# One weight tile of a decode kernel, loaded in 16 pieces of 1 to 15 and 8 partitions

## The chip, the cores and the metric

The kernel runs on one core of one Trainium2 chip. The metric is the device time of one execution in microseconds (us). Three runs of the kernel before gave 1349.16, 1345.97 and 1348.38 us; their median is 1348.38 us. In the text PE is TensorE, PEld its weight load, DVE VectorE, ACT ScalarE, POOL GpSimd and SP SyncE, whose queue issues nearly all DMAs of this kernel. A DMA is carried out by the core's 16 DMA engines.

## The reference

One decode step of a transformer block for two sequences: attention against a cache of 8192 positions, then a bilinear feed-forward block. All tensors are float32. Cut to what matters:

```python
# B, D, H, Sk, Dh, F = 2, 448, 16, 8192, 256, 1792
q = (layernorm(x) @ wq).reshape(B, 1, H, Dh).transpose(0, 2, 1, 3)
p = softmax(einsum("bhqd,bhkd->bhqk", q, k_cache) * Dh ** -0.5)
o = einsum("bhqk,bhkd->bhqd", p, v_cache)
h = x + o.transpose(0, 2, 1, 3).reshape(B, 1, H * Dh) @ wo
out = h + ((layernorm(h) @ w_gate) * (layernorm(h) @ w_up)) @ w_down
```

The two caches hold 2 x 16 x 8192 x 256 numbers each, 537 MB together. They are read once.

## The kernel before, in words

The loop over `i` takes the 32 pairs of a head `h` and a sequence `b` one after the other (`h, b = divmod(i, 2)`). Each step reads two tiles of K (`k_h_b_0`, `k_h_b_1`) and two of V (`v_h_b_0`, `v_h_b_1`). Such a tile has 128 partitions with 32 KB each, 4 MB in all. The four tiles of a step live in four buffers (`ring`), so a tile of step `i` takes the buffer of the same tile of step `i - 1`: a K tile can be issued when DVE has scanned the K tile before it, a V tile when PE has multiplied with the V tile before it.

DVE scans each K tile with 32 multiply-and-sum instructions (L203) against the query, which stands broadcast on all partitions. The softmax of the 8192 scores goes over PE, DVE and ACT in small instructions (L212 to L227: `m`, `mT`, `nm`, `nb_ps`, `p`, `l_ps`, `rl`). PE then multiplies the 64 columns of `p` with the two V tiles (L234, `o_ps`; 16 products of two columns for each tile), and projects the head's result into `acc_ps` (L252).

The weights come by head pairs: `w_hp` holds, for two heads, the rows of `wq` and `wo`, as 128 partitions with 3584 numbers (14,336 bytes) each, 1.8 MB in all. `load_w` (L138) fetches one; there are two buffers for it. `w_0` is loaded first of all, and `w_{hp+1}` is issued in the step in which `hh == 1 and b == 0`, between that step's K loads and its V loads (L195). The last one, `w_7`, belongs to step 26 (`h` = 13, `b` = 0). The queries of the next head pair are computed from it in the same step by 10 matmuls, which the trace shows as 20 (L173 and L178, `queries`), and are first needed in step 28.

All loads of K, V and weights go through SP's one queue in program order. SP issues a load and goes on; where a load has to wait (for its buffer, or for a counter), SP waits, and everything behind it in the program waits too. The scheduler gives each load one of eight completion counters (`DMAHW0` to `DMAHW7`), in turn, and a load is not issued until the load that had the same counter before it, eight loads earlier, has landed. The order of PE's, DVE's and ACT's instructions is set by the scheduler from the program. After the loop, `wg_t`, `wu_t` and `wd_t` (the feed-forward weights, 6.9 MB, in the freed buffers) are loaded, and a tail of PE, DVE and ACT work of some 10 us follows the landing of `wu_t`.

Of the kernel before, what the change touches and what calls it, by code (L numbers as in the profile page):

```python
# [13 lines left out]
B, D, H, SK, DH, F = 2, 448, 16, 8192, 256, 1792  # L14
EPS = 1e-5
P = 128
# [9 lines left out]
FG = (512, 512, 384, 384)  # L26
FO = (0, 512, 1024, 1408)
NF = F // P

LAYOUT = (  # L30
    (slice(0, P), slice(0, DC - 1), slice(0, DC - 1)),
# [6 lines left out]
def tile_decode_block(  # L38
# [18 lines left out]
    nc = tc.nc  # L57
# [79 lines left out]

    def load_w(hp):  # L138
        t = wpool.tile([P, WQ + WO], F32, tag="w", name=f"w_{hp}")
        nc.sync.dma_start(t, wqo[hp])  # L140
        return t

    def load_cache(src, b, h, c, name):
# [3 lines left out]
        return t  # L147

    w_now = load_w(0)

    xT = transposed(x_sb, "x")
# [39 lines left out]
    for i in range(H * B):  # L191
        h, b = divmod(i, B)
        hp, hh = divmod(h, 2)
        kt = [load_cache(k_cache, b, h, c, "k") for c in range(NCH)]
        if hh == 1 and b == 0 and hp + 1 < H // 2:  # L195
            w_next = load_w(hp + 1)
# [63 lines left out]
    def load_ff(w, name):  # L260
        t = ring.tile([P, NF * D], F32, tag="ring", name=name)
        nc.sync.dma_start(t, w)
        return t
# [3 lines left out]

    wd_t = ring.tile([P, NF, D], F32, tag="ring", name="wd_t")
    at = 0
# [60 lines left out]
    for g in range(4):  # L330
        for n in range(FG[g] // P):
            for q in range(DC):
                nc.tensor.matmul(  # L333
                    y_ps[32 * q : 32 * q + B, : DW[q]], hmT[:, n, g, :],
                    wd_t[:, k, q * P : q * P + DW[q]],
                    start=False, stop=(k == NF - 1),
                )
# [14 lines left out]
def pack(np, inputs):  # L352
# [20 lines left out]
    a = np.asarray(inputs["B_w_down"])  # L373
    got["wd"] = a.reshape(NF, P, D).transpose(1, 0, 2).reshape(P, NF * D)
    return {k: np.ascontiguousarray(v) for k, v in got.items()}
# [25 lines left out]
```

## Time and profile before

| | us |
|---|---|
| runs: lowest, median, highest | 1345.97, 1348.38, 1349.16 |
| the profiled execution: its span, first to last instruction | 1345.7 |
| PE busy | 496.5 |
| DVE busy | 741.2 |
| ACT busy | 60.6 |
| moved from memory | 561.2 MB, a mean of 418 GB/s |

The profiled execution has a span of 1345.7 us; no other time of it is given, and its span lies 2.7 us under the median of the runs. The profile page shows the busy time of each engine, the span in 40 slices, the DMA queues, the chain of work that ended last, and the costliest groups of instructions. Apart from the page, the trace answers questions: the chain in order of time, the instructions of one engine in a stretch of time, and, for given stretches, each engine's busy time with the mean busy share of the 16 DMA engines and the rate that they reached in GB/s. One DMA engine of 16 is a share of 0.0625.

### The profile page before, as it was taken

How to read it: one execution, taken by the hardware profiler on the slowest of the kernel's cores; microseconds unless marked ns; L12 is line 12 of the kernel's file. 1: busy time of each engine (PE TensorE's matmuls, PEld its weight loads, DVE VectorE, ACT ScalarE, POOL GpSimd, SP SyncE). 2: the span in 40 equal slices, each digit the busy share in tenths (PEclk: the TensorE clock that was granted, in tenths of full speed). 3: DMA queues.
4: the chain of work that ended last, by engine and by line, in shares of the span. 5: the costliest groups of instructions: out<-in, count | busy, mean ns of one | idle time of the engine just before them, and what ended most of it. 6: DMA issues, size and time to landing. Idle time of an engine off the chain costs nothing.

```text
span 1345.7 us, 10677 instructions
## 1 busy us (share of the span) xinstructions
PE 496.5 (37%) x2892; PEld 165.4 (12%) x2892; DVE 741.2 (55%) x4232; ACT 60.6 (5%) x182; POOL 1.2 (0%) x8
## 2 busy tenths in 40 slices
PE   3344223462224532155331533325343342333217
PEld 1111001120001210011100111101011020111003
DVE  5555664446654366653466634566444665445661
ACT  0000000000000000000000000000000000000000
POOL 0000000000000000000000000000000000000000
PEclk8667676675666865668655677656766576766569
DMA  9999999999999999999999999999999999999994
GB/s 405 428 433 430 433 429 430 431 430 433 432 426 433 430 432 432 428 433 430 425 412 417 430 433 408 411 411 430 430 407 412 413 435 426 411 407 414 417 404 189
DMA packets 20520, 561.87 MB, mean 418 GB/s; under 512 B 2280, under 2 KB 2412, under 8 KB 2668
## 3 DMA queue, kind: packets, MB, share of 16 engines
q1 hardware_dynamic: 20452, 561.20, 98.2%
q8 instruction: 22, 0.36, 0.1%
q14 instruction: 38, 0.31, 0.1%
q10 hardware_dynamic: 8, 0.00, 0.0%
HBM read 561.19 MB, written 0.00 MB: 417 GB/s over the span
## 4 chain that ended last, share of the span: by engine, by line
DMA 71%; DVE 27%; PE 1%; issue 1%; DVEq 0%; ACT 0%; SPq 0%
DMA k<-in_A_k_cache_dram 70%; DVE junk L203 27%; DMA wu_t<-in_B_w_up_dram 2%; PE u_ps L299 0%; PE y_ps L333 0%; DVE hm L323 0%; PE hm_ps L326 0%; DVEq L203 0%; DVE y L345 0%; ACT y L343 0%; SPq L140 0%; DVE hmT L328 0%; DVEq L323 0%
## 5 line engine op out<-in xcount | busy, mean ns | idle before, releaser
L203 DVE SCALAR_TENSOR_TENSOR junk<-k,q 128x256 f32<-128x256 f32 x2048 | 710.9, 420 | 483.6 <-DMA k<-in_A_k_cache_dram 483.6
L234 PE MATMUL o_ps<-v,p 128*2 128x512 f32 x2048 | 297.4, 741 | 37.2 <-DMA v<-in_A_v_cache_dram 37.0
L214 PE MATMUL mT<-ident,m 128*1 128x128 f32 x32 | 11.2, 351 | 624.0 <-DVE m L212 624.0
L203 DVE DVE_READ_ACCUMULATOR junk<-k,q 128x1 f32 x2048 | 168.2, 82 | 0.0
L173 PE MATMUL q_ps<-w,xb 128*128 128x512 f32 x96 | 60.7, 783 | 105.9 <-DMA w<-in_wqo_dram 104.5
L234 PEld LDWEIGHTS o_ps<-v,p 128*2 128x2 f32 x2048 | 53.5, 97 | 251.6 <-issue 197.7
L214 PEld LDWEIGHTS mT<-ident,m 128*1 128x1 f32 x32 | 2.6, 81 | 634.0 <-DVE m L212 613.5
L243 PE MATMUL oT_ps<-sel,o_sb 128*128 128x1 f32 x256 | 33.7, 253 | 23.2 <-ACT o_sb L239 23.2
L173 PEld LDWEIGHTS q_ps<-w,xb 128*128 128x128 f32 x96 | 23.6, 256 | 140.6 <-DMA w<-in_wqo_dram 114.7
L227 DVE RECIPROCAL rl<-l_ps 128x1 f32<-128x1 f32 x32 | 5.4, 169 | 62.9 <-PE l_ps L225 62.9
L252 PE MATMUL acc_ps<-w,oT 128*2 128x448 f32 x64 | 35.8, 695 | 5.6 <-ACT oT L249 5.6
L243 PEld LDWEIGHTS oT_ps<-sel,o_sb 128*128 128x128 f32 x256 | 31.0, 191 | 53.1 <-ACT o_sb L239 53.1
L220 ACT ACTIVATE nb<-nb_ps 128x1 f32<-128x1 f32 x32 | 5.5, 171 | 671.2 <-PE nb_ps L218 671.2
L239 ACT ACTIVATE o_sb<-o_ps 128x512 f32<-128x512 f32 x32 | 19.1, 597 | 353.7 <-PE o_ps L234 353.7
L225 PE MATMUL l_ps<-lsum,ones 128*128 128x1 f32 x64 | 17.3, 340 | 24.9 <-ACT p L223 24.9
L218 PE MATMUL nb_ps<-nm,row 1*128 1x1 f32 x64 | 16.7, 328 | 13.4 <-DVE nm L216 13.4
L216 DVE TENSOR_REDUCE nm<-mT 1x1 f32<-1x128 f32 x32 | 8.9, 279 | 20.4 <-PE mT L214 20.4
L183 ACT ACTIVATE q<-q_ps 128x512 f32<-128x512 f32 x16 | 9.6, 597 | 193.5 <-PE q_ps L178 193.5
L225 PEld LDWEIGHTS l_ps<-lsum,ones 128*128 128x128 f32 x64 | 14.6, 283 | 27.6 <-ACT p L223 27.6
L218 PEld LDWEIGHTS nb_ps<-nm,row 1*128 1x128 f32 x64 | 14.5, 280 | 23.1 <-issue 12.4
L178 PE MATMUL q_ps<-w,xb 128*128 128x256 f32 x64 | 16.5, 380 | 0.0
L178 PEld LDWEIGHTS q_ps<-w,xb 128*128 128x128 f32 x64 | 12.5, 195 | 9.5 <-issue 8.6
(74 smaller groups left out, 74.9 us busy)
## 6 DMA issues: line engine op xcount, KB each, us to landing
k<-in_A_k_cache_dram SPq DMA_DIRECT2D x64, 4096.0 KB, 28.6
v<-in_A_v_cache_dram SPq DMA_DIRECT2D x64, 4096.0 KB, 34.7
w<-in_wqo_dram SPq DMA_DIRECT2D x8, 1792.0 KB, 31.5
wg_t<-in_B_w_gate_dram SPq DMA_DIRECT2D x1, 3136.0 KB
wu_t<-in_B_w_up_dram SPq DMA_DIRECT2D x1, 3136.0 KB, 23.9
wd_t<-in_wd_dram SPq DMA_DIRECT2D x1, 1792.0 KB, 19.7
wd_t<-in_wd_dram SPq DMA_DIRECT2D x1, 672.0 KB, 21.0
wd_t<-in_wd_dram SPq DMA_DIRECT2D x1, 448.0 KB, 21.7
```

The lines of the kernel that those rows point to most:

```text
L173: nc.tensor.matmul(ps, xb[:, c, b, :], w[:, c * 2 * DH : (c + 1) * 2 * DH], start=(c == 0), stop=False,)
L178: nc.tensor.matmul(ps[:, k * DH : (k + 1) * DH], xb[:, DC - 1 + k, b, :], w[:, 3 * 2 * DH : WQ], start=False, stop=(k == 1),)
L183: nc.scalar.activation(q.rearrange("p h d -> p (h d)"), ps, AF.Copy)
L203: nc.vector.scalar_tensor_tensor(junk[j % 4], kt[c][:, j, :], 1.0, q_now[b][:, hh, :], op0=ALU.mult, op1=ALU.mult, accum_out=s[:, col : co ...
L214: nc.tensor.transpose(mT, m, ident)
L216: nc.vector.tensor_reduce(nm, mT, axis=AX.X, op=ALU.max, negate=True)
L218: nc.tensor.matmul(nb_ps, row, nm, start=True, stop=True)
L225: nc.tensor.matmul(l_ps, ones, lsum, start=True, stop=True)
L234: nc.tensor.matmul(o[g : g + 2, :], p[:, 2 * t : 2 * t + 2], vt[c][:, j : j + 2, :], start=(t < 4), stop=(t >= NJ // 2 - 4),)
L239: nc.scalar.activation(o_sb, o, AF.Copy)
L243: nc.tensor.matmul(oT_ps[:, c : c + 1], o_sb[:, (2 * k + c) * P : (2 * k + c + 1) * P], sel[:, k : k + 1], start=(k == 0), stop=(k == 1),)
L252: nc.tensor.matmul(acc_ps, oT[:, c, :], w_now[:, WQ + (hh * 2 + c) * D : WQ + (hh * 2 + c + 1) * D], start=(h == 0 and c == 0), stop=(h == ...
```

## The change

`load_w` for the last head pair issues 16 loads in place of one. They take 1, 2, 3 and so on to 15 partitions, and then the remaining 8: 120 + 8 = 128 partitions, each with its full 14,336 bytes. The bytes, the tile and its place in the program stay. The other seven loads of weights are as before.

```diff
+RULER = (*range(1, 16), 8)
...
     def load_w(hp):
         t = wpool.tile([P, WQ + WO], F32, tag="w", name=f"w_{hp}")
-        nc.sync.dma_start(t, wqo[hp])
+        at = 0
+        for n in RULER if hp == H // 2 - 1 else (P,):
+            nc.sync.dma_start(t[at : at + n], wqo[hp, at : at + n])
+            at += n
         return t
```

The change moves instructions at two places, both in step 26. In the lists, a row is one issue or a group of like instructions, with the counters or engines that it waits for.

On SP's queue, where `w_7` stands between the K and the V loads of step 26, before:

```order
L146 DMA k_13_0_0_3686<-in_A_k_cache_dram 128x8192 [waits DMAHW5_49,DVE_49]
L146 DMA k_13_0_1_3688<-in_A_k_cache_dram 128x8192 [waits DMAHW6_49,DVE_49]
L140 DMA w_7_3690<-in_wqo_dram 128x3584
L146 DMA v_13_0_0_3692<-in_A_v_cache_dram 128x8192 [waits DMAHW7_49,PE_49]
L146 DMA v_13_0_1_3694<-in_A_v_cache_dram 128x8192 [waits DMAHW0_49,PE_49]
```

and now, from its seventh small load on:

```order
L145 DMA w_7_3690<-in_wqo_dram 7x3584 [waits DMAHW1_49]
L145 DMA w_7_3690<-in_wqo_dram 8x3584 [waits DMAHW2_49]
L145 DMA w_7_3690<-in_wqo_dram 9x3584 [waits DMAHW3_49]
L145 DMA w_7_3690<-in_wqo_dram 10x3584 [waits DMAHW4_49]
L145 DMA w_7_3690<-in_wqo_dram 11x3584 [waits DMAHW5_49]
L145 DMA w_7_3690<-in_wqo_dram 12x3584 [waits DMAHW6_49]
L145 DMA w_7_3690<-in_wqo_dram 13x3584 [waits DMAHW7_49]
L145 DMA w_7_3690<-in_wqo_dram 14x3584 [waits DMAHW0_49]
L145 DMA w_7_3690<-in_wqo_dram 15x3584 [waits DMAHW1_49]
L145 DMA w_7_3690<-in_wqo_dram 8x3584 [waits DMAHW2_49]
L152 DMA v_13_0_0_3707<-in_A_v_cache_dram 128x8192 [waits DMAHW3_49,PE_49]
L152 DMA v_13_0_1_3709<-in_A_v_cache_dram 128x8192 [waits DMAHW4_49,PE_49]
```

Before, the load of `w_7` waited for nothing. Now the first four small loads wait for nothing, and the fifth to the sixteenth each wait for the load that stands eight places ahead of them in this queue: the seventh for `k_13_0_0`, the eighth (8x3584, the first of the two) for `k_13_0_1`, the ninth for the first small load, and so on; `v_13_0_0` now waits for the ninth small load as well as for PE.

On PE, where the queries of `w_7` stand near the softmax of step 26, before:

```order
L173 MATMUL q_ps_7_0_3761<-w_7_3690,xb_138 128x512 [waits DMAHW3_49]
L173 MATMUL q_ps_7_0_3761<-w_7_3690,xb_138 128x512 x2
L178 MATMUL q_ps_7_0_3761<-w_7_3690,xb_138 128x256 x2
L173 MATMUL q_ps_7_1_3769<-w_7_3690,xb_138 128x512 x3
L178 MATMUL q_ps_7_1_3769<-w_7_3690,xb_138 128x256 x2
L214 MATMUL mT_26_3779<-ident_82,m_26_3777 1x128 [waits DVE_49]
L218 MATMUL nb_ps_26_3783<-nm_26_3781,row_91 128x1 [waits DVE_49]
L225 MATMUL l_ps_26_3790<-lsum_26_3788,ones_87 128x1 [waits Activation_49]
L234 MATMUL o_ps0_103<-v_13_0_0_3692,p_26_3787 2x512 [waits DMAHW4_49]
```

and now:

```order
L220 MATMUL mT_26_3794<-ident_82,m_26_3792 1x128 [waits DVE_49]
L224 MATMUL nb_ps_26_3798<-nm_26_3796,row_91 128x1 [waits DVE_49]
L231 MATMUL l_ps_26_3805<-lsum_26_3803,ones_87 128x1 [waits Activation_49]
L179 MATMUL q_ps_7_0_3776<-w_7_3690,xb_138 128x512 [waits DMAHW4_49,DMAHW5_49,DMAHW3_49,DMAHW6_49,DMAHW2_49,DMAHW7_49,DMAHW1_49,DMAHW0_49]
L179 MATMUL q_ps_7_0_3776<-w_7_3690,xb_138 128x512 x2
L184 MATMUL q_ps_7_0_3776<-w_7_3690,xb_138 128x256 x2
L179 MATMUL q_ps_7_1_3784<-w_7_3690,xb_138 128x512 x3
L184 MATMUL q_ps_7_1_3784<-w_7_3690,xb_138 128x256 x2
L240 MATMUL o_ps0_103<-v_13_0_0_3707,p_26_3802 2x512 [waits DMAHW3_49]
```

The queries of the last head pair stood ahead of the small matmuls of the softmax of step 26 and now stand behind them, still ahead of the products with `v_13_0_0`; they wait for all eight counters in place of one. Line numbers from L140 on grow by 5 or 6.

## The prediction

> **What bounds the kernel now.** I read the page's queues first, then the chain of waits in order of time, then the DMA rate in chosen stretches.
>
> The page's DMA part, with the number of packets and the share of 16 DMA engines' time for each queue:
>
> ```profile
> q1 hardware_dynamic: 20452, 561.20, 98.2%
> q10 hardware_dynamic: 8, 0.00, 0.0%
> k<-in_A_k_cache_dram SPq DMA_DIRECT2D x64, 4096.0 KB, 28.6
> w<-in_wqo_dram SPq DMA_DIRECT2D x8, 1792.0 KB, 31.5
> x_sb<-in_A_x_dram ACTq DMA_DIRECT2D x1, 3.5 KB
> ```
>
> The DMA engines are busy 98.2% of the span; nothing else is near it. The packets also tell how a load is divided. SP's queue has 142 loads of 128 partitions (64 K, 64 V, 8 weights, 6 feed-forward) and one store of 2. If each partition is a packet and each engine taking part adds one at the end, that is 142 x (128 + 16) + (2 + 2) = 20,452, which is the row. The two 2-partition loads on the other queue give 2 x (2 + 2) = 8, also the row. So a full load gives 8 partitions to each of 16 engines, and a load of two occupies two engines. I take it that a load of n occupies n, one partition each.
>
> The chain, in order of time; a row is start, length, what. K tiles landing set the pace, in the middle of the run:
>
> ```profile
> 519.88 28.54 DMA k<-in_A_k_cache_dram
> 559.70 28.57 DMA k<-in_A_k_cache_dram
> 599.54 32.82 DMA k<-in_A_k_cache_dram
> 643.63 28.55 DMA k<-in_A_k_cache_dram
> ```
>
> A step takes 559.70 - 519.88 = 39.82 us, and one with a weight load 643.63 - 599.54 = 44.09. The difference, 4.27 us, is the price of 8 packets of 14,336 bytes on an engine: 0.533 us each. From the changed step on:
>
> ```profile
> 1053.28 29.00 DMA k<-in_A_k_cache_dram
> 1082.37 10.62 DVE junk L203 x61
> 1093.56 32.85 DMA k<-in_A_k_cache_dram
> 1137.61 28.67 DMA k<-in_A_k_cache_dram
> 1177.56 29.15 DMA k<-in_A_k_cache_dram
> 1217.98 29.29 DMA k<-in_A_k_cache_dram
> 1258.55 28.73 DMA k<-in_A_k_cache_dram
> 1309.62 23.90 DMA wu_t<-in_B_w_up_dram
> ```
>
> Steps are a little longer here: 39.95, 40.42 and 40.57 us. Last, the rate in three stretches (the last two columns are the mean busy share of the 16 engines and GB/s):
>
> ```profile
> 1084.00:1088.00 4.00, 0.00 (x0) 0.00 (x0) 4.00 (x25) 0.00 (x0) 0.00 (x0) 0.52 1.00 434
> 1328.00:1338.00 10.00, 7.63 (x67) 2.95 (x66) 2.33 (x11) 0.69 (x1) 0.00 (x0) 1.00 0.06 27
> 1338.00:1341.00 3.00, 2.63 (x80) 2.26 (x83) 0.22 (x2) 0.00 (x0) 0.00 (x0) 1.00 0.09 29
> ```
>
> This is the key to the kernel. At the end a share of 0.06, one engine of 16, is still moving data for 13 us after the others have stopped, at 27 GB/s, and wu_t, for which PE waits until 1333.52, is among what it brings. **One DMA engine is late**, and a tile has landed only when its part is in. When all 16 move, a 4 MB tile takes 4.194 MB / 434 GB/s = 9.66 us, four take 38.66; but a step takes 39.8 to 40.6. So the other 15 have 1.2 to 1.9 us to spare in each step, and the late one has none. Which of the 16 it is, no view shows, nor how late it is at 1093; I take about the 13 us of the end.
>
> **The change part by part.** SP's rows around the place (start, length, what; x2 are two issues with the wait between them), and PE's:
>
> ```profile
> 1064.73 0.43 SPq L140 DMA_DIRECT2D w<-in_wqo_dram  x1
> 1072.55 4.02 SPq L146 DMA_DIRECT2D v<-in_A_v_cache_dram  x2
> 1097.30 4.79 PE L173 MATMUL q_ps<-w,xb 128*128 128x512 f32 x6 [17.32 <-DMA w<-in_wqo_dram]
> 1106.22 0.27 PE L214 MATMUL mT<-ident,m 128*1 128x128 f32 x1
> 1108.29 3.62 PE L234 MATMUL o_ps<-v,p 128*2 128x512 f32 x32
> ```
>
> *The issues.* Fifteen more at 0.43 us are 6.5 us of SP, which by itself is hidden: SP stands idle between 1065.2 and 1072.5. *The waits are not.* The eighth small load waits for k_13_0_1. Its neighbour k_13_0_0 lands at 1053.28 + 29.00 = 1082.3, one tile more gives 1092, and DVE's scan of it follows at 1093.5 without a gap, so I put it at 1093. Before, V was issued at 1072.55; now SP stands until 1093, and behind it stand eight more small loads, both V tiles of the step (for which PE waits) and the next K (for which DVE waits; its buffer is free only at 1093.56 anyway). The first seven small loads are out by then and lie behind k_13_0_1; the 15 fast engines have nothing else and run dry, while the late one works on k_13_0_1 until 1093 in any case. So the hold costs the path nothing before 1093; what counts is how soon after it V starts.
>
> *The nine held loads* (8 to 15 and 8 partitions, 100 packets), from 1093 on. The first lanes of every load are the same engines if a load of n takes the first n, so some engines carry nine packets. Lower bound: packets at the full load's pace, 9 x 0.533 = 4.8 us, and 1.0 from an issue to its first byte. Upper bound: one packet at a time, as if one engine's 27 GB/s were all there is, 100 x 0.533 = 53 us. The trace has one load of few partitions to go by:
>
> ```profile
> 0.73 0.54 ACTq L69 DMA_DIRECT2D x_sb<-in_A_x_dram  x1
> 2.88 0.45 PE L132 MATMUL T_ps_x<-ident,x_sb 2*128 2x2 f32 x3 [2.88 <-DMA x_sb<-in_A_x_dram]
> ```
>
> From its issue to its use it took 2.15 us. A small load here is held by an earlier small one and then moves neighbouring partitions at once, so I price it like that row, which lies between the ends: 9 x 2.15 = 19.4 us. The weights are complete at 1093 + 19.4 = 1112.4, against 1097.3: **15.1 us later**.
>
> [...] The row for free packets is the full load's: 0.533 us on all 16 engines at once. [...]
>
> *V and K after it.* Engines with a packet of every small load start v_13_0_0 some 15 us later than before, and all tiles behind it move by as much. PE's new order hides behind that: the small softmax matmuls no longer wait for the weights, the queries (1097.30 to 1106.22, 8.9 us) run from 1112.4 to 1121.3, and v_13_0_0 lands at 1112.4 + 9.7 = 1122.1. Without that cover, o_ps would start at about 1082.37 + 2 x 11.2 (two scans) + 2.1 (mT to o_ps) + 8.9 = 1115.8 in place of 1108.3.
>
> *What comes back.* At 1093 the fast engines' lead is gone, since they have run dry, and then those of them with a packet of every small load fall behind the late one, unless that is itself among them. From there on they set the pace, at 38.66 us a step. Four steps from 1093.56 to 1258.55 took 165.0 - 4.27 = 160.7 us, at the fast engines' pace 154.6; the fifth (28.73 + 10.62 + 0.6, about 40.0) gives 1.3. In all 6.1 + 1.3 = 7.4 us come back.
>
> Sum: 15.1 - 7.4 = **+7.7 us**. The profiled execution goes from 1345.7 to 1353.4. The median of the runs lies 2.7 above that execution, so 1348.4 + 7.7 = 1356.1.
>
> **The rivals.** *Small packets at full pace* (the lower bound). The engines are through at 1093 + 1.0 + 4.8 = 1098.8, and V starts there in place of 1097.3: +1.5. The pause lets the fast engines fall back level with the late one, and steps may return from 40.2 to the 39.82 of mid-run, five times 0.35 = -1.8. Together nothing: 1348. For it speaks the 434 GB/s of full loads; against it that no small load of the trace shows such a pace.
>
> *Faster: the late engine is spared.* If it is one that carries none of the small loads, it saves its 8 packets, -4.27 us, and this counts if V is issued before it is through with k_13_0_1 at 1093, so that it runs on without a pause: 1344.1. The 0.06 rows speak for it, since only one engine's work matters. Against it is SP's order: V stands behind the eighth small load, which waits for that very engine, so V's first byte comes at 1093 + 9 x 0.43 + 1.0 = 1097.9 at best, and the spared 4.27 is spent waiting. [...] The trace agrees that one is late and cannot name it.
>
> *One after another* (the upper bound): 53 + 1 in place of 4.27, less 7.4: +42, 1391. For it speaks only that each load may wait for an earlier one; but up to eight may be out at a time.
>
> **How the numbers follow.** Forecast 0.66, full pace 0.24, spared 0.06, one after another 0.04. Within the forecast, the late engine among the first seven means that little comes back: +15, 1363.5, the top of the range. At the bottom, full pace with the regained steps and some luck of the spared engine, 1347. So 1347 to 1363.5; what is left out is the fourth case, most of the third, and the wings. Faster or slower means here by over 0.3%, 4.0 us, about what this kernel's runs can tell apart. Slower: 0.60 from the forecast (0.06 of it comes back nearly whole) and 0.04 from the fourth, 0.64. Same: 0.24 + 0.06 = 0.30. Faster: 0.06.
>
> **What would show it.** Packets on SP's queue: 141 x 144 + 4 + 2 x 128 = 20,564 if a load of n runs on n engines (the one-partition load split over 16 would make it 30 more); far from that, the dividing is wrong. SP issues v_13_0_0 not at 1072 but after 1095. The DMA share between 1083 and 1095 falls far below 1. The queries start at about 1112 (forecast) or before 1101 (full pace). The stretch with one engine at the end, 13 us now, shrinks or is gone if the others are the late ones; then steps after 1140 take under 39.5 us. If instead the steps stay at 40 and the lone engine stays at the end, nothing came back, and the time is 1363. If V's issue does not move, the waits were misread.

## The result and the profile after

The changed kernel takes 1360.81 us (median of four runs, 1359.59 to 1362.32), the kernel before, beside it, 1347.18 us (1345.78 to 1349.16). The ratio is 1.0102, with a 95% interval of 1.0087 to 1.0118: **slower by 13.7 us**. Here and below a difference in us is the ratio's, times the median of the kernel before. The profiled executions differ by 11.9 us, 1357.6 against 1345.7 of span, and the readings below are made against these two.

The page of the changed kernel: its span, busy times with the number of instructions, and two DMA queues:

```profile
span 1357.6 us, 10695 instructions
PE 501.1 (37%) x2892; PEld 167.2 (12%) x2892; DVE 741.1 (55%) x4232; ACT 60.6 (4%) x182; POOL 1.3 (0%) x8
q1 hardware_dynamic: 20564, 561.20, 97.7%
q14 instruction: 38, 0.31, 0.1%
```

The packets of q1, SP's queue, are the 20,564 of the forecast; 2386 of them have 4 bytes, 112 more than before (2274), which is 128 for the sixteen small loads in place of 16 for the one. So I count one such packet for each engine that takes part, and a small load of n partitions runs on n DMA engines. Next SP's own instructions around the place (start, length, what, count; a group's length includes the waits within it):

```profile
1052.66 11.39 SPq L152 DMA_DIRECT2D k<-in_A_k_cache_dram  x2
1064.11 34.60 SPq L145 DMA_DIRECT2D w<-in_wqo_dram  x16
1099.68 1.64 SPq L152 DMA_DIRECT2D v<-in_A_v_cache_dram  x2
1102.78 2.78 SPq L152 DMA_DIRECT2D k<-in_A_k_cache_dram  x2
```

The sixteen issues stretch over 34.60 us, and V follows at 1099.68 where it was at 1072.55. What the DMA engines did meanwhile stands in the last two columns of these windows, their mean busy share and GB/s (a packet counts in the window in which it starts, so a share can come out above 1):

```profile
1084.00:1088.00 4.00, 0.00 (x0) 0.00 (x0) 4.00 (x25) 0.00 (x0) 0.00 (x0) 0.50 0.06 25
1088.00:1092.00 4.00, 0.00 (x0) 0.00 (x0) 4.00 (x25) 0.00 (x0) 0.00 (x0) 0.50 0.05 18
1092.00:1096.00 4.00, 0.00 (x0) 0.00 (x0) 4.00 (x25) 0.00 (x0) 0.00 (x0) 0.50 0.38 87
1096.00:1100.00 4.00, 0.00 (x0) 0.00 (x0) 4.00 (x25) 0.00 (x0) 0.00 (x0) 0.50 0.81 147
1100.00:1104.00 4.00, 0.00 (x0) 0.00 (x0) 4.00 (x25) 0.00 (x0) 0.00 (x0) 0.50 1.15 135
1104.00:1108.00 4.00, 1.39 (x5) 1.01 (x5) 1.70 (x10) 0.61 (x3) 0.00 (x0) 0.50 0.95 123
1112.00:1116.00 4.00, 4.00 (x6) 1.42 (x6) 0.00 (x0) 0.00 (x0) 0.00 (x0) 0.50 0.91 393
1348.00:1350.00 2.00, 1.28 (x10) 0.12 (x2) 0.57 (x1) 0.00 (x0) 0.00 (x0) 1.00 0.06 25
```

From 1084 to 1092 one engine of 16 works. Then comes the more telling part: from 1096 to 1108 the engines are busy nearly all the time, at 123 to 147 GB/s instead of 434. They are hardly waiting for work; their packets take about three times as long (a median of 1.49 us for the 14,336 bytes of a held packet, where one of a full load takes 0.535). The last row shows that one engine is still alone at the end of the run. PE in the same stretch (in brackets: idle time before, and what ended it):

```profile
1105.51 0.37 PE L220 MATMUL mT<-ident,m 128*1 128x128 f32 x1 [24.22 <-DVE m L218]
1111.56 5.46 PE L179 MATMUL q_ps<-w,xb 128*128 128x512 f32 x6 [3.40 <-DMA w<-in_wqo_dram]
1121.26 3.61 PE L240 MATMUL o_ps<-v,p 128*2 128x512 f32 x32
1130.58 5.28 PE L240 MATMUL o_ps<-v,p 128*2 128x512 f32 x32 [5.70 <-DMA v<-in_A_v_cache_dram]
```

The weights are complete at 1111.56, 14.3 us later than before (1097.30). The chain of waits, its DMA rows from there on, with DVE's scan of k_13_0_1 ahead of them:

```profile
1094.05 8.73 DVE junk L209 x51
1102.78 37.46 DMA k<-in_A_k_cache_dram
...
1151.44 28.64 DMA k<-in_A_k_cache_dram
...
1191.28 28.62 DMA k<-in_A_k_cache_dram
...
1231.17 28.52 DMA k<-in_A_k_cache_dram
...
1270.97 28.57 DMA k<-in_A_k_cache_dram
...
1321.88 23.72 DMA wu_t<-in_B_w_up_dram
```

The next K tile lands at 1102.78 + 37.46 = 1140.24, before at 1126.41: **13.8 us lost**. From there the steps take 39.84, 39.89 and 39.80 us, where they took 39.95, 40.42 and 40.57, and wu_t lands at 1345.60 against 1333.52: 12.1 later. So only some **1.8 us came back** by then, and 11.9 are left at the end.

The packet records behind the DMA rows add one thing that no view groups: what the lone engine of 1084 to 1094 did. Each row is a start in us, a length in ns, bytes and queue; the records do not name the engine:

```
1084.99  1361  32768  q1
1086.35  1214  32768  q1
1087.56  1214  32768  q1
1088.77  1214  32768  q1
1089.98   333   8192  q14
1090.30  1875  32768  q1
1092.17  1213  32768  q1
1093.39   541  14336  q1
1093.93   535  14336  q1
1094.47   540  14336  q1
1095.01   622  14336  q1
```

It finishes its part of k_13_0_1 at 1093.38 and then goes through four small packets one after the other, which I read as its share of the first seven small loads (from 1094.74 on the other engines move packets too). If a load of n takes the first n engines, the loads of 4, 5, 6 and 7 partitions give one to the fourth; the third would have five and the fifth three. The experiments below test this. And between its K packets stands a packet of another queue, q14, which the page calls "instruction": it costs 333 ns, and the K packet behind it 1875 - 1213 = 662 more, together 1.0 us.

### The profile page after: what moved, and what is told of

It is laid out like the page before. It is cut to its first block, busy times and chain, and to the rows that moved or that the text cites. A ratio compares the mean times of both kernels' runs of the same rounds, so it can differ in the third digit from the quotient of the medians.

```text
span 1357.6 us, 10695 instructions
## 1 busy us (share of the span) xinstructions
PE 501.1 (37%) x2892; PEld 167.2 (12%) x2892; DVE 741.1 (55%) x4232; ACT 60.6 (4%) x182; POOL 1.3 (0%) x8
## 3 DMA queue, kind: packets, MB, share of 16 engines
q1 hardware_dynamic: 20564, 561.20, 97.7%
## 4 chain that ended last, share of the span: by engine, by line
DMA 71%; DVE 28%; PE 1%; issue 1%; DVEq 0%; ACT 0%; SPq 0%
DMA k<-in_A_k_cache_dram 69%; DVE junk L209 27%; DMA wu_t<-in_B_w_up_dram 2%; PE u_ps L305 0%; PE y_ps L339 0%; DVE hm L329 0%; PE hm_ps L332 0%; DVEq L209 0%; DVE y L351 0%; ACT y L349 0%; SPq L145 0%; DVE hmT L334 0%; DVEq L329 0%
## 5 line engine op out<-in xcount | busy, mean ns | idle before, releaser
L179 PE MATMUL q_ps<-w,xb 128*128 128x512 f32 x96 | 64.3, 823 | 99.9 <-DMA w<-in_wqo_dram 98.5
```

The costliest lines, as they stand in the source:

```text
L179: nc.tensor.matmul(ps, xb[:, c, b, :], w[:, c * 2 * DH : (c + 1) * 2 * DH], start=(c == 0), stop=False,)
```

## The experiments

Three questions: what makes the held loads slow, whether the wait is free before 1093, and which engine is late, and why. All ratios are to the kernel before on the same chip.

### Neighbouring partitions or the loads themselves

**ruler_stride8** keeps the sixteen sizes, their order and their waits, but each load takes every eighth partition, so that no two packets of a load go to neighbouring partitions.

```diff
+RULER = (*((n, n - 1) for n in range(1, 9)),
+         *((16 - n, n - 1 + 8 * n) for n in range(7, 0, -1)), (8, 7 + 8 * 8))
...
-        nc.sync.dma_start(t, wqo[hp])
+        for n, at in RULER:                      # last head pair
+            rows = slice(at, at + 8 * (n - 1) + 1, 8)
+            nc.sync.dma_start(t[rows], wqo[hp, rows])
```

> The same 16 loads of the last weight tile in the same order, with the same sizes and waits; only the partitions differ: a load takes every eighth partition in place of neighbouring ones. [...] If a small load costs some 2 us for its issue, its wait and its landing whatever it writes (theory B), nothing changes against the changed kernel: 13 to 14 us slower than before.

Measured: 1355.78 us, ratio 1.0054 (1.0034 to 1.0073), 7.3 us slower. Its SP rows, and the two waits for K in its chain:

```profile
1064.63 37.33 SPq L152 DMA_DIRECT2D w<-in_wqo_dram  x16
1102.07 0.86 SPq L158 DMA_DIRECT2D v<-in_A_v_cache_dram  x2
```

```profile
1064.26 30.77 DMA k<-in_A_k_cache_dram
...
1103.03 33.95 DMA k<-in_A_k_cache_dram
```

The same waits hold V as long as before (1102.07 against 1099.68), but the next K tile lands at 1136.98, 3.3 us earlier than in the changed kernel, and PE's queries started at 1109.09 without waiting for weights. In the packet records four of five held 14,336-byte packets take 0.82 to 1.25 us here (median 1.03), 0.92 to 1.93 in the changed kernel (median 1.49). From the issue of the eighth small load to the end of the last small packet it is 11.0 us here (1095.04 to 1106.05) and 16.6 in the changed kernel (1093.86 to 1110.46). So neighbouring or spaced partitions account for a part of the loss: 6.4 of 13.7 us by the runs, 3.5 of 11.9 by the two spans (1357.6 and 1354.1). The spacing has a price of its own, which this difference holds too: SP is 0.6 to 0.8 us busy with each spaced held load, and 0.27 to 0.37 with each held load of neighbours. A spaced load also reads rows that lie apart in memory; the kernel extra_3 below bears on that.

**first_tile_adjacent** and **first_tile_apart** move the question to the start of the run, where no late engine and no K tile is in the way: the first weight tile comes in 16 loads of 8 partitions, neighbours or four apart.

```diff
+        if hp == 0:
+            for g in range(16):                               # adjacent
+                nc.sync.dma_start(t[8 * g : 8 * g + 8], wqo[hp, 8 * g : 8 * g + 8])
+            return t
...
+                at = 32 * (g // 4) + g % 4                    # apart
+                rows = slice(at, at + 29, 4)
+                nc.sync.dma_start(t[rows], wqo[hp, rows])
```

> The disputed cost by itself, at the start, where the DMA engines are idle and no engine is late: the FIRST weight tile in 16 loads of 8 neighbouring partitions, the last one in one load as before. Each load runs on 8 engines, 16 packets each. [...] Theory B (about 2 us a load, whatever the partitions): with up to eight loads in flight, the same 30 or so here and in the run with partitions four apart. [...]

> The same 16 loads of 8 partitions for the first weight tile, but the 8 partitions of a load lie four apart. [...] Theory B: as slow as the run with neighbouring partitions.

Measured: 1370.06 us, ratio 1.0178 (1.0151 to 1.0204), and 1354.52 us, ratio 1.0068 (1.0047 to 1.0088); 23.9 and 9.1 us slower. Two windows and PE's first queries, with neighbours:

```profile
4.00:8.00 4.00, 0.40 (x2) 0.32 (x2) 0.49 (x3) 0.00 (x0) 0.00 (x0) 1.00 0.58 75
24.00:28.00 4.00, 0.00 (x0) 0.00 (x0) 0.00 (x0) 0.00 (x0) 0.00 (x0) 1.00 0.99 98
```

```profile
33.70 5.46 PE L177 MATMUL q_ps<-w,xb 128*128 128x512 f32 x6 [23.76 <-DMA w<-in_wqo_dram]
```

and four apart, with SP's first rows:

```profile
4.00:8.00 4.00, 1.21 (x5) 1.00 (x4) 1.94 (x10) 0.26 (x1) 0.00 (x0) 1.00 0.45 147
```

```profile
15.94 4.29 PE L179 MATMUL q_ps<-w,xb 128*128 128x512 f32 x6 [9.14 <-DMA w<-in_wqo_dram]
```

```profile
0.73 10.84 SPq L144 DMA_DIRECT2D w<-in_wqo_dram  x16
11.61 0.91 SPq L152 DMA_DIRECT2D k<-in_A_k_cache_dram  x2
```

From 4 to 8 us hardly anything but these loads is under way: neighbours reach 75 GB/s at a share of 0.58, which is 129 for a full share, and four apart 147 at 0.45, which is 327. The later window with neighbours, 98 GB/s at 0.99, holds K packets too, and those are slow as well. In the packet records a 14,336-byte packet of the first tile takes a median of 1.73 us with neighbours and 0.56 four apart, next to 0.535 in a full load. That the second kernel is still 9.1 us slower lies with SP: its sixteen issues take 0.68 us each and put the first K issue at 11.61, where it was at 1.19 before, and nothing hides them at the start. A load of neighbours keeps SP busy for only about 0.3 us (0.27 to 0.37 for a held one of the changed kernel), so part of this is the price of the spacing.

### Is the wait free before 1093?

**eight_by_16** loads the last tile in eight loads of 16 neighbours. Only the eighth is held, so nearly all of the nine held loads are gone.

```diff
+RULER = (16,) * 8
...
+        for n in RULER if hp == H // 2 - 1 else (P,):
+            nc.sync.dma_start(t[at : at + n], wqo[hp, at : at + n])
+            at += n
```

> The last weight tile in 8 loads of 16 neighbouring partitions: every engine has 8 packets as before, the eighth load and the V loads behind it are still held until k_13_0_1 has landed at about 1093, but only one small load is left behind the hold. If the hold itself costs the path nothing, because the late engine is busy until 1093 in any case (theory A): within 2 us of before, V issued at about 1094, and the steps behind it at 39.8 us. If holding V for 20 us is what costs (theory B): 8 to 14 us slower.

Measured: 1355.95 us, ratio 1.0053 (1.0037 to 1.0068), 7.1 us slower. The waits for K in its chain:

```profile
1063.41 35.13 DMA k<-in_A_k_cache_dram
...
1100.21 34.31 DMA k<-in_A_k_cache_dram
```

It came out slower than one theory and less slow than the other. The reason lies ahead of the wait, for the most part: k_13_0_1 lands at 1063.41 + 35.13 = 1098.54. In the changed kernel SP issued the load that waits for it at 1093.86. While the fifteen early engines move their small packets, the late engine's K packets take up to 3.9 us instead of 1.21.

Two more kernels ask whether that, too, is a matter of neighbouring partitions. **eight_spaced** takes every eighth partition; **port_spared** keeps neighbours, but leaves the eight partitions 12 to 15 and 44 to 47 for the end.

```diff
+        for g in range(8):                                    # eight_spaced
+            rows = slice(g, P, 8)
+            nc.sync.dma_start(t[rows], wqo[hp, rows])
...
+EARLY = ((0, 12), (32, 44), *((a, a + 16) for a in (16, 48, 64, 80, 96, 112)))
+        for a, z in (*EARLY, (12, 16), (44, 48)):             # port_spared
+            nc.sync.dma_start(t[a:z], wqo[hp, a:z])
```

> The last weight tile in 8 loads of 16 partitions, as in eight_by_16, but each load takes every eighth partition (0, 8, 16 and so on, then 1, 9, 17), so that no more than two of its packets fall on one group of four neighbours. Only the eighth load is held, for k_13_0_1. [...] Rival B (eight small loads ahead of the late engine's K cost it by their number, wherever they write): as eight_by_16, 6 to 8 us over the kernel before.

> The last weight tile in ten loads: eight of 12 or 16 neighbouring partitions (0 to 11, 32 to 43, 16 to 31, 48 to 63 and so on to 127), which leave out the partitions 12 to 15 and 44 to 47, and then these in two loads of 4. Seven are issued ahead of the wait for k_13_0_1, and the eighth, ninth and tenth behind it. [...] Rival B (early small loads slow the late engine by their number or bytes, wherever they write): k_13_0_1 lands at 1097 to 1099 and the time is 5 to 9 us over the kernel before.

Measured: eight_spaced 1351.8 us, ratio 1.004 (1.0026 to 1.0055), 5.4 us slower; port_spared 1354.72 us, ratio 1.0066 (1.005 to 1.0081), 8.9 us slower. The wait for k_13_0_1 in the chain of the first:

```profile
1062.56 34.75 DMA k<-in_A_k_cache_dram
```

and of the second:

```profile
1062.98 33.86 DMA k<-in_A_k_cache_dram
```

Landings at 1097.31 and 1096.84: both kernels that send some hundred small packets past the late engine make it some five or six microseconds late, wherever the packets go. (The time of eight_spaced, 5.4, lies a little under the 6 to 8 of its rival B; its landing is as late as B has it.) So the slowing of a K packet by small packets on other engines did not go away with a choice of the partitions that these write. That the eight partitions left out in port_spared bear on the late engine was an assumption of mine; no run shows it, and leaving them out did not help. In the packet records the late engine was through with k_13_0_1 at 1092.49 before; counted from each kernel's own K issue, it is 1.5 us later with the 24 early packets of the changed kernel, 2.2 with the 24 of ruler_stride8, and 5.3 to 6.5 with the 97 to 105 of these three. That fits a delay by their number, some 0.06 us each; where they meet stays open.

### Which engine is late, and why

**extra_3** and **extra_4** are the kernel before with one more small load in every step, into a scratch tile that nothing reads, of 3 or 4 partitions (0, 4, 8 and 12).

```diff
+    scr = const.tile([P, WQ + WO], F32, name="scr")
...
+        nc.sync.dma_start(scr[0 : 4 * 3 : 4], wqo[0, 0:3])    # extra_4: 4 * 4 and 0:4
```

> The kernel before with one more load in each of the 32 steps, between the K and the V loads: 3 partitions of 14,336 bytes into an unused tile, at partitions 0, 4 and 8. If the late engine is the fourth of the 16 (theory A), the first three engines take these packets in the 1 us per step that they have to spare: 0 to 2 us slower. If the late engine is one of the first three: about 32 x 0.53 = 17 us slower.

> The same with 4 partitions (0, 4, 8 and 12), so that the fourth engine takes a packet too. Theory A (the fourth engine is the late one): 32 x 0.53 = 17 us slower than before, while the load of 3 costs 0 to 2. If the late engine is a later one: 0 to 2 us, like the load of 3.

Measured: 1345.53 us, ratio 0.9989 (0.9979 to 0.9999), and 1364.64 us, ratio 1.0126 (1.0104 to 1.0149). Packets of extra_3 and of extra_4:

```profile
q1 hardware_dynamic: 20644, 562.57, 98.4%
```

```profile
q1 hardware_dynamic: 20708, 563.03, 97.8%
```

The rows are 32 x (3 + 3) and 32 x (4 + 4) above 20,452. Ninety-six packets on the first three engines cost nothing; thirty-two more on the fourth cost 17.0 us, 0.53 each, the price of one packet. **The late engine is the fourth**, the one that takes the fourth packet of a small load. The packet records of extra_4 show it directly: the fourth packet of the extra load starts 2.2 us after the first in the second step, 5.1 in the fifth and 10.0 in the tenth, so this engine falls back by about 1 us a step.

The packet records of extra_3 answer the rival of the spaced loads. An extra load of three reads three rows that follow one another and writes partitions four apart, and from the second step on, outside the steps with a weight tile, each of its 72 packets takes 0.535 to 0.540 us, as in a full load. Reading neighbouring rows alone does not slow a packet, then; this was seen with three rows at a time, not with fifteen.

What makes it late, I suspected, is the q14 packet of the record above, which I took for a piece of some engine's instructions. DVE has 4232 of them, and the next kernels give DVE fewer: part of each K tile's scan is done in chunks of eight columns, one multiply over 8 x 256 numbers and one sum, instead of 8 instructions with a read-out each. **dve_half_chunked** does this for half of a tile, **dve_chunked** for all of it.

```diff
+            for j in range(16, JC, 8):                        # dve_chunked: range(0, JC, 8)
+                nc.vector.tensor_mul(prod, kt[c][:, j : j + 8, :],
+                    q_now[b][:, hh, None, :].to_broadcast([P, 8, DH]))
+                nc.vector.tensor_reduce(s[:, col : col + 8], prod, axis=AX.X, op=ALU.add)
-            for j in range(JC):
+            for j in range(16):                               # dve_chunked: range(0)
```

> The kernel before with half of each K tile's 32 DVE scans done as two multiplications over 8 rows each with two sums, so a step has about 74 DVE instructions in place of 134. Theory: the late engine is late because it also fetches the instructions of one compute engine, once in a step, for about 1 us; with about half the DVE instructions that is 0.55 us, and steps go from 39.8 to about 39.4: 10 to 16 us faster than before. If the lateness has nothing to do with DVE's instructions: no change, or slower by what DVE's longer scan (about 14 in place of 11 us a tile) costs.

> All of each K tile's scan done in multiplications over 8 rows with a sum each: 16 DVE instructions a step in place of 128. Theory: the fetches all but vanish, steps go to 38.7 to 39.0 us and the one engine at the end is gone: 20 to 32 us faster than before, if DVE's scan (about 17.6 us a tile, 35 a step) stays within the step. Rival: DVE becomes the bound or its longer scan delays the next K, and the gain is lost.

Measured: 1340.15 us, ratio 0.9954 (0.9938 to 0.997), 6.2 us faster, and 1360.08 us, ratio 1.0116 (1.0089 to 1.0142), 15.6 us slower. The page of the half-chunked kernel:

```profile
PE 507.1 (38%) x2892; PEld 170.1 (13%) x2892; DVE 949.2 (71%) x2440; ACT 60.6 (5%) x182; POOL 1.2 (0%) x8
q14 instruction: 23, 0.19, 0.0%
```

and of the fully chunked one:

```profile
PE 491.2 (36%) x2892; PEld 165.0 (12%) x2892; DVE 1199.4 (88%) x648; ACT 60.6 (4%) x182; POOL 1.2 (0%) x8
q14 instruction: 10, 0.08, 0.0%
DVE 77%; DMA 14%; PE 5%; issue 2%; ACT 1%; DVEq 0%; ACTq 0%
```

The changed kernel, like the one before, has 4232 DVE instructions and 38 packets on q14. From 4232 to 648 instructions q14 loses 28 packets, one for every 128, and 4232 to 2440 takes 15: by this count 33 of the 38 packets on q14 go with DVE's instructions, and some five do not. The fully chunked kernel shows the other side: DVE's scan takes longer, and now DVE is 77% of the chain.

The half-chunked kernel gained less than the 10 to 16 us expected. Its longer scans stand in the way at both ends: the first step's scan releases the next K load at 32.85, before at 29.07, and the end of the chain goes through the last step's o_ps instead of wu_t. So the last two kernels chunk only steps 2 to 29, **dve_half_middle** half of a tile and **dve_three_quarters_middle** three quarters.

```diff
+            alone = 16 if 1 < i < H * B - 2 else JC           # three quarters: 8
+            for j in range(alone, JC, 8):
...
+            for j in range(alone):
```

> The kernel before (the last weight tile in one load) with half of each K tile's scan in chunks of 8 columns, as in dve_half_chunked, but in steps 2 to 29 alone; the first two and the last two steps scan as before. Theory A (each instruction fetch of DVE costs the late engine about 1 us, and dve_half_chunked lost some 3 us at the start and some 3 us at the end, because its scans are longer): 1332 to 1338, lower than the 1340.15 of dve_half_chunked. Rival B (the gain of dve_half_chunked came from something else, or the longer scans cost in every step): 1340 to 1342.

> As dve_half_middle, with three quarters of each K tile's scan in chunks of 8 columns: in the middle steps 2 x (8 x 0.42 + 6 x 2.28) = 34.1 us of scan a step plus the softmax. Theory A: still fewer fetches, so steps of 38.9 to 39.3, and a time of 1328 to 1336 as long as DVE keeps up. Rival B (DVE becomes the bound, as it did in dve_chunked with 42 us a step): steps above 39.8 and a time over 1340.

Measured: 1333.49 us, ratio 0.9899 (0.9884 to 0.9913), and **1324.73 us, ratio 0.9836 (0.9821 to 0.985)**, 22.1 us faster than the kernel before, a little more than expected, and the fastest of all. The second one's page and some steps of its chain:

```profile
PE 496.1 (37%) x2892; PEld 168.7 (13%) x2892; DVE 1014.5 (77%) x1880; ACT 60.6 (5%) x182; POOL 1.2 (0%) x8
q14 instruction: 19, 0.16, 0.0%
```

```profile
679.66 22.69 DMA k<-in_A_k_cache_dram
718.44 22.81 DMA k<-in_A_k_cache_dram
757.34 28.01 DMA k<-in_A_k_cache_dram
801.44 22.76 DMA k<-in_A_k_cache_dram
840.36 23.66 DMA k<-in_A_k_cache_dram
880.12 22.83 DMA k<-in_A_k_cache_dram
```

Steps are now of two kinds: 718.44 to 757.34 is 38.90, 840.36 to 880.12 is 39.76 us. The packet records show the difference. Of the twenty steps without a weight load from 156.86 to 1202.51, seven take 39.73 to 39.89 us, and each of them holds a q14 packet; thirteen take 38.77 to 38.92, and eleven of these hold none (the other two hold three that cost nothing; not all of q14 is DVE's). So a step without a fetch runs near the pace of the fast engines (38.66 by the forecast), and one with a fetch is about a microsecond longer. Before, every step had at least one q14 packet.

## Why the prediction came out as it did

The forecast, 1353.4 for the profiled execution and 1356.1 for the runs, was right in sign and in how the time is lost, and wrong in how much of it comes back; the time came 4.2 and 4.7 us above it.

- **How a load is divided:** right to the packet, 20,564.
- **The issues and the waits:** right. V went from 1072.55 to 1099.68, forecast as after 1095; the share between 1084 and 1092 fell to one engine.
- **"The hold costs the path nothing before 1093":** nearly right for this ruler, 1.5 us instead of 0, which I put down to the 24 early small packets. It is not a rule: with about a hundred of them the late engine came 5 to 6 us late.
- **The nine held loads, 19.4 us (bounds 4.8 and 53):** SP issues the first of them at 1093.86 and the weights are complete at 1111.56, so 17.7 us, 1.97 a load for the 2.15 of the x_sb row. The path lost 13.8 us for the forecast 15.1. The size was right and the picture only in part: the loads did not follow one another. SP issued all nine within 4.6 us (the last at 1098.43), and most of the 17.7 us are the nine packets that each of the first eight engines has, stretched to a median of 1.49 us. That the x_sb row, one load of two small packets, gives nearly the same is luck. What a small load of large packets to neighbouring partitions costs, no load of the kernel before showed; the runs did: the 1.49 us for 0.535, and the same loads with spaced partitions cost 7.3 us where these cost 13.7. Why neighbours slow each other was not shown. What the 7.3 are made of was not taken apart: the wait stays, a spaced issue is longer, and packets there still take 1.03 us for 0.535.
- **PE's new order:** hidden, as forecast. The queries ran from 1111.56 to 1121.3 (forecast 1112.4 to 1121.3), and o_ps followed without a wait for its first V tile.
- **"What comes back", 7.4 us: the step that failed.** 1.8 came back. The condition stood in the text, "unless that is itself among them": the late engine, the fourth, has a packet of every load of 4 partitions or more, so 13 of them instead of 8, and of all nine held ones. So the others did not fall behind it. It went on losing about 1.0 us a step, which fits engines that were nearly level after the hold: five and a half more steps give the lone stretch of the end. The steps went to 39.84, the pace of mid-run, instead of 38.66, and at the end one engine was again alone, for some 6 us instead of 13. The 1.8 us is only what the last steps before had above 39.82, which the forecast had put into its second case.
- **The sum:** measured 13.8 - 1.8 - 0.1 = 11.9; with the failed term set to this, the forecast's own would have been 15.1 - 1.8 = 13.3. The case in the range's top, nothing back and 1363.5, is close to the 1360.81 that came.
- **The rivals:** *full pace* would have had the nine loads in 4.8 us and the queries before 1101. *The spared engine* fell with the same fact as the term above: it carries nearly every small load. *One after another* needed 53 us for 100 packets; it took 17.7.

## What to carry to other kernels

Before splitting a load into small ones, ask which partitions each writes: here packets to neighbouring partitions stretched to about three times their length (medians of 1.49 us in the changed kernel and 1.73 in first_tile_adjacent, for 0.535 in a full load), and this shows as busy DMA engines at a low rate (123 to 147 GB/s at shares of 0.81 to 1.15, for 434 at 1.00). Partitions four apart kept their pace (0.56 us), but each such issue kept SP busy twice as long (0.68 us for about 0.3), and every split kernel here was slower than the one load, by 5.4 to 23.9 us. Before counting on time coming back behind a stall, find out which DMA engine sets the pace and whether it carries the stalled work; two kernels with one more small load of 3 and of 4 partitions told it here. And where a kernel is bound by its DMA engines, the number of instructions of an engine that is not the bottleneck can cost time: fewer and longer DVE instructions (1880 for 4232) gave 1.6% in dve_three_quarters_middle.

## What the runs showed of the hardware that I had not expected

- The number of DVE instructions shows in the DMA packets: on q14, which the page calls "instruction", 4232 of them go with 38 packets, 2440 with 23, 1880 with 19 and 648 with 10, so one packet of 8192 bytes for about 128. In the kernel before such a packet takes 0.31 to 0.33 us, and the 32,768-byte packet that follows it at once takes 1.75 to 1.88 us in 33 of the 38 cases, where the median of such packets is 1.21. In the lone stretch of the changed kernel it stands among the packets of the late engine, and with 19 in place of 38 the kernel was 22.1 us faster. So I read it as a fetch of DVE's instructions through the fourth engine, which at one a step, about 1.0 us, paces the run.
- A packet of 14,336 bytes in a small load takes 0.56 us when the load's partitions lie four apart, 1.03 when they lie eight apart and 1.73 when eight of them are neighbours (medians of first_tile_apart, ruler_stride8's held loads and first_tile_adjacent; the three differ in load size and in what else is moving; why eight apart is slower than four apart was not tested).
- Small loads issued ahead of a wait can delay the very load that the wait is for: while small packets ran on the fifteen other engines, the late engine's K packets took up to 3.9 us in eight_by_16, for 1.21, and k_13_0_1 landed at 1098.54, where the wait for it ended by 1093.86 in the changed kernel. Where these packets meet was not found.
